# The eighth block's convolution in the short form, the permuted input weights loaded two blocks earlier, a row buffer cleared later

## The chip, the cores and the metric

The kernel runs on one core of a Trainium2 chip. A core has five engines that each work through their own instructions in order and meet at semaphores: TensorE (PE in the profile; PEld is its loading of weights), VectorE (DVE), ScalarE (ACT), GpSimd (POOL), and SyncE (SP), which here only issues DMAs. GpSimd issues DMAs too. Matrix products land in PSUM, from where ScalarE and VectorE carry them to SBUF. The metric is the device time of one execution in microseconds, the median over several runs.

## The reference

Two stages on 8 x 4096 tokens of 192 features (8 heads of 24). First a causal convolution whose 7 taps are given per token and head, after a softmax over the taps; then a two-layer network of width 2048 with a squared ReLU:

```python
w = softmax(weight_gen)                      # (B, S, 8 heads, 7 taps)
x_unf = x_pad[:, idx, :].reshape(B, S, 7, 8, 24)
y = einsum('bshk,bskhg->bshg', w, x_unf).reshape(B * S, 192)
h = maximum(y @ w_in, 0)                     # 32768 x 2048
out = (h * h) @ w_out                        # 32768 x 192
```

The result is float32; inside, the kernel computes in float16 with float32 sums.

## The kernel before

**Tiling.** The 32768 tokens are 64 tiles of 512. They go in 33 blocks (`BLOCKS`, L55), counted from 0: blocks 0 and 1 are one tile, all others two (block 7 is tiles 12 and 13). Batch row 1 begins with tile 8.

**Stages of a block.**

1. *Softmax.* Tap weights are worked on in parts of a batch row: eight, sixteen or thirty-two tokens on each of 128 partitions (`PARTS`, L102). A part is loaded (`load`, L209), then goes through in pieces: an exponential on ScalarE (`exp`, L239), and on VectorE a sum, a reciprocal and four or eight products into a row buffer (`soft`, L841, which calls `total`, `recip` and `scale`). Small parts use `v_first`, the others `v_big` (L103), in which each token's taps stand on the diagonal of an 8-token square and all else is zero; it must be cleared once before its first use. When a part's last piece is done, a small part is moved straight to the tiles' rows `wr` by DMAs on two queues (`move_rows`, L684); a larger one is stored to DRAM (`store`, L285) and loaded again as rows (`wr_load`, L354), which has to wait for the store.
2. *Bands.* `st_bands` (L665) multiplies a tile's rows by a mask on VectorE and makes a band matrix `bd` (some 2.3 us per tile).
3. *Convolution.* TensorE multiplies x by the bands. The long form (`st_conv`, L525) takes 120 matmuls, because heads of 24 features straddle groups of 32; both PSUM results are copied by ScalarE. The short form (`st_conv_spread`, L488) gives each of six heads its own group of 32 and puts the last two heads' features into the holes: 80 matmuls, one copy on ScalarE and one on VectorE, and then four small DMAs on SyncE that move rows within y (L523). The input weights then have to stand in the matching order: `w_p` in place of `w_i`. `FIRST_SPREAD` (L48) says from which block on the short form is used.
4. *Units.* `st_unit` (L578): 16 units u0 to u15 for each block, six matmuls each into a PSUM buffer; ScalarE applies ReLU, VectorE squares, two units at a time but for u14 and u15, which are squared singly (L603).
5. *Second product.* `st_mm2` (L618) in steps, eight a block (M0 to M7), each 32 matmuls over eight of the sixteen units. They lag: the steps in block j use the units of block j-1. An even step begins a pair of accumulators in PSUM, the odd one after it ends them, and `o_sum` (L646) brings them out: ScalarE copies one, VectorE adds the other. There is a single pair (`ps_o`, one buffer, L90), so the next even step can begin only when that sum is done. An odd M step reads units 8 to 15, the last of them at its end.

PSUM has three more buffers (`ps_h`, L89), which the units and both halves of a convolution take in turn.

**What sets the order.** Everything is emitted in an order written out by hand, and each engine keeps it. For blocks 0 to 3 the whole order is in `plans` (L762); for later blocks it comes from a pattern of letters: u is a unit, M a second-product step, C the convolution of the next block. The pattern is `steady` (L760) before a long convolution, `steady_spread` (L761) before a short one:

```python
steady = "MuMuuu" * 3 + "MuuuMCu"
steady_spread = "MuMuuu" * 2 + "MuCMuuu" + "MuMuuu"
```

Into it are put, each ahead of a given unit, softmax pieces (S, from `TIMES`, L779, as block and unit), their exponentials (E, `exp_time`, L788), loads (L) and bands (B, L811 to L818). What is ahead of u12 in the order is thus ahead of u12's square on VectorE. In plan 3, S3 ends the fourth part of batch row 0, and S4 begins the first part of row 1; B6 and B7 are block 4's bands.

**GpSimd's queue.** It holds the x loads (issued behind the convolution that frees their buffer, L896 to L900), half of the row moves (L368), the loads of `w_p` (`load_w_spread`, L151, 16 DMAs, in block 5 behind its x loads), two DMAs that cross the halves of `w_p` (`cross_w_spread`, L175, in block 6), and, in the opening, the memset of `v_big` (L755) between the x loads of tiles 2 and 3.

Of the kernel before, what the change touches and what calls it, by code (L numbers as in the profile page):

```python
# [9 lines left out]
def kernel(  # L10
# [26 lines left out]
    nc = tc.nc  # L37
# [7 lines left out]
    HK = H * KK  # L45
    G = D // H
    SPREAD = H - 2
    FIRST_SPREAD = 8  # L48
    HP = H // 2

    P = 128
# [51 lines left out]
    v_big = const.tile([P, R + 2 * HALO, HP, SL, 2], f16, name="v_big")  # L103
# [43 lines left out]
    def cross_w_in(q):  # L147
        for r0, r1 in ((0, RT), (RT, 0)):
            nc.sync.dma_start(out=w_i[r0 : r0 + RT, q, 1], in_=w_i[r1 : r1 + RT, q, 0])

    def load_w_spread():  # L151

        def rows(head, k=None):
            a = moe_w_in[G * head : G * (head + 1)]
            return a if k is None else a.rearrange("(r k) c -> k r c", k=NK)[k]

        for e in (0, 1):
            for k in range(NK):
                for a, n, src in (
                    (0, G, rows(2 * k + e)), (G, RT // 2 - G, rows(SPREAD + e, k))  # L160
                ):
                    if k < 2:
                        p0 = RT * k + 32 * e + a
                        nc.gpsimd.dma_start(
                            out=w_p[p0 : p0 + n, :, 0, 0:NQ],
                            in_=src.rearrange("r (q c) -> r q c", q=WQ),
                        )
                    else:
                        for half in (0, 1):
                            p0 = RT * half + 32 * e + a  # L170
                            nc.gpsimd.dma_start(
                                out=w_p[p0 : p0 + n, :, 0, NQ:],
                                in_=src.rearrange("r (q h c) -> h r q c", q=WQ, h=2)[half],
                            )
    def cross_w_spread():  # L175
        for r0, r1 in ((0, RT), (RT, 0)):
            nc.gpsimd.dma_start(out=w_p[r0 : r0 + RT, :, 1], in_=w_p[r1 : r1 + RT, :, 0])
# [158 lines left out]
    def x_load(j):  # L336
        x_t[j] = p_x.tile([P, NT, D], f16, name="xt")
        block_load(j, x_t[j], x[j // NBB], D, nc.gpsimd)
# [149 lines left out]
    def st_conv_spread(j):  # L488

        s0, n = BLOCKS[j]  # L490
        y = p_y.tile([P, NK + 1, TB], f16, name="y")
        y_t[j] = y
        for ks in ((NK, NK - 1), (0, 1)):
            yp = ps_h.tile([P, 2, TB], f32, name="yp", tag="h")
            k0 = min(ks)
            for k in ks:
                for i in range(NT):
                    a, b = bounds[i], bounds[i + 1]
                    for half in (0, 1):
                        s = s0 + half  # L500
                        hi = a + (STEP if tile_start(s, i) == starts[i] else b - a)
                        bd = bd_t[s][:, H * a : H * hi].rearrange(
                            "p (g c e) -> p g e c", g=HP, e=2
                        )
                        for e in (0, 1):
                            head = 2 * k + e
                            p0 = RT * half + 32 * e
                            c0 = min(G * head, D - 32)
                            nc.tensor.matmul(  # L509
                                out=yp[p0 : p0 + 32, k - k0, a:b],  # L510
                                lhsT=x_t[s][:, i, c0 : c0 + 32],
                                rhs=bd[:, head // 2, e, 0 : b - a],
                                start=True,
                                stop=True,
                                skip_group_check=True,
                                tile_position=(0, p0),
                            )
            copy = nc.vector.tensor_copy if k0 == 0 else nc.scalar.copy
            copy(out=y[:, k0 : k0 + 2], in_=yp)  # L519
        for p0 in range(0, P, 32):  # L520
            head = SPREAD + p0 // 32 % 2
            r0 = p0 + G * head - min(G * head, D - 32)
            nc.sync.dma_start(out=y[p0 + G : p0 + 32, 0:NK], in_=y[r0 : r0 + G, NK])  # L523

    def st_conv(j):  # L525

        if j >= FIRST_SPREAD:
            return st_conv_spread(j)
# [49 lines left out]
    def st_unit(j, u):  # L578

        w = w_p if j >= FIRST_SPREAD else w_i  # L580
        h = ps_h.tile([P, 2, TB], f32, name="h", tag="h")
# [83 lines left out]
    def st_bands(j):  # L665
        first = int(j % NBB == 0)
        last = NT - int(tile_start(j, NT - 1) != starts[-1])
        split = 2 if j == BLOCKS[NFIRST][0] else first
        for tiles in (range(first), range(first, split), range(split, last), range(last, NT)):
            if tiles:  # L670
                st_band(j, tiles)

    with nc.allow_low_precision("fp16 matmul pipeline"), tc.manual_schedule():
# [69 lines left out]
        def cast_w_in(e, copy):  # L743
# [8 lines left out]

        s2.load(nc.gpsimd)
        x_load(2)
        nc.gpsimd.memset(v_big, 0.0)  # L755

        steady = "MuMuuu" * 3 + "MuuuMCu"  # L760
        steady_spread = "MuMuuu" * 2 + "MuCMuuu" + "MuMuuu"  # L761
        plans = {  # L762
            0: "E1 u B1 u u u C S1 u u M u u",
            1: "L3 u u B2 M E2 B3 u u M E2 u S2 S2 u M u C u M",
            2: "L4 u u u E3 M u u u M B4 u u u u M B5 S3 u u u u M u C u",
            3: "L5 L6 u u E3 u M S3 u u u M u M E4 u u B6 u M u M B7 u u u E4 M u M C S4 u",
        }


# [3 lines left out]
        def at(j, u, kind, *args):  # L773
            fill.setdefault((j, u), []).append((kind, *args))
# [4 lines left out]
        TIMES = {  # L779
            (1, 0): ((3, 15), (4, 0)),  # L780
            (1, 1): ((4, 15), (5, 0)),
            (1, 2): ((4, 2), (5, 1), (5, 15)),
            (2, 0): ((6, 1), (6, 15), (7, 0)),
            (2, 1): ((7, 9), (8, 9)),
            (3, 0): ((9, 9), (10, 0), (10, 9), (11, 9)),
# [2 lines left out]
        def exp_time(j, u):  # L788

            if u == 0:  # L790
                return j - 1, 12
            return j, {1: 0, 2: 1, 7: 3, 8: 4, 9: 4, 13: 12, 15: 8}[u]

        for n, s in enumerate(parts):
            k = n - min(m for m, p in enumerate(parts) if p.b == s.b)
# [15 lines left out]
        for j in range(len(plans), NBLK - 1):  # L811
            a = BLOCKS[j + 1][0]
            small = [p for p in parts if p.fb <= j + 1][-1].r == FIRST
            us = {4: (7, 9), 6: (7, 9)}.get(j, (5, 9) if small else (1, 5))
            if j + 1 >= FIRST_SPREAD:
                us = (1, 5)
            for n, u in enumerate(us):
                at(j, u, "B", a + n)  # L818
        for j in range(len(plans), NBLK):
            plan, u = [], 0  # L820
            for step in steady_spread if j + 1 >= FIRST_SPREAD else steady:
                if step == "u":
                    plan += [f"{kind}{n}" for kind, n in fill.get((j, u), ())]
                    u += 1
                plan.append(step)
            plans[j] = " ".join(plan)
# [3 lines left out]
        def load_rows(j):  # L830

            s = [p for p in parts if p.fb <= j][-1]
            if s.r == FIRST:
                return
            if s in stored:
                for n in range(BLOCKS[j][0], sum(BLOCKS[j])):
                    wr_load(n)
            else:
                waiting.append((s, j))
# [40 lines left out]
        for j in range(NBLK):  # L880
            if j + 2 < NBLK:
                load_rows(j + 2)
            if j == 1:
                for q in range(WQ):
                    cross_w_in(q)
            u = 0
            for step in plans[j].split():
                kind, n = step[0], int(step[1:] or 0)
                if kind == "u":
                    st_unit(j, u)  # L890
                    u += 1
                elif kind == "M":
                    next(mm2)
                elif kind == "C" and j + 1 < NBLK:
                    st_conv(j + 1)
                    if j == 0:  # L896
                        x_load(3)
                    elif j + 2 < NBLK:
                        for k in range(BLOCKS[j + 2][0], sum(BLOCKS[j + 2])):
                            x_load(k)  # L900
                    if j == 5:
                        load_w_spread()
                    elif j == 6:
                        cross_w_spread()
                elif kind == "E":
                    parts[n].exp(*next(parts[n].exps))
                elif kind == "S":
                    soft(parts[n])
                elif kind == "B":
                    st_bands(n)  # L910
                elif kind == "L":
                    parts[n].load(nc.sync)


        j = NBLK - 1
# [44 lines left out]
```

## Time and profile before

| what | before |
|---|---|
| median of 6 runs | 730.03 us (729.86 to 732.21) |
| profiled execution | 730.17 us, its span 728.5 us |
| TensorE matmuls busy | 722.3 us, 99% of the span |
| weight loads busy | 530.9 us, 73% |
| VectorE busy | 625.8 us, 86% |
| ScalarE busy | 612.5 us, 84% |
| GpSimd busy | 99.5 us, 14% |
| granted TensorE clock | 0.999 of full speed |
| memset of the big row buffer | 2.49 us, from 17.65 us on |
| 6 long convolutions, matmuls | 120 each, in blocks 1 to 6 |
| 25 short convolutions, matmuls | 80 each, from 153.7 us on |

A line of the timeline has start, time, engine, source line, operation, what it writes and reads, shape and count; in brackets, how long the engine stood idle before it and what ended that. Instructions that follow each other alike are merged into one line. Times of one instruction overlap the next one's a little, so what an instruction costs its engine is best read from start to start. A busy TensorE in the table is not TensorE at its peak: ends of matmuls are modelled. Block 6 runs from 118.6 to 141.1 us, block 7 to 163.2.

### The profile page before, as it was taken

The page shows a single profiled execution, that of the slowest core. Times are in us where ns is not written, and L with a number is a line of the kernel's source. Part 1 is how long each engine was busy: PE and PEld are TensorE (multiplying, and loading weights), DVE is VectorE, ACT ScalarE, POOL GpSimd, SP SyncE. Part 2 cuts the span into 40 slices and gives each one's busy share as a digit, 9 for nine tenths or more (in the row PEclk, how much of TensorE's full clock was granted, in tenths as well). Part 3 has the DMA queues.
Part 4 walks back from the last instruction along what each step waited for, and adds up shares of the span by engine and source line. Part 5 has one row for each costly group of instructions (what it writes and reads, how often), then busy time and mean ns, then how long its engine had stood idle before and what let it go on. Part 6 is the DMA issues. An engine that isn't in the chain of part 4 may idle for free.

```text
span 728.5 us, 31057 instructions
## 1 busy us (share of the span) xinstructions
PE 722.3 (99%) x14082; PEld 530.9 (73%) x14082; DVE 625.8 (86%) x839; ACT 612.5 (84%) x731; POOL 99.5 (14%) x147
## 2 busy tenths in 40 slices
PE   8999999999999999999999999999999999999998
PEld 6668877777777777777777777777777777777777
DVE  7989997998898998888988888988888988778753
ACT  6898888888888888888888888888888888888883
POOL 6331223411001100011001010010000110001000
PEclk9999999999999999999999999999999999999999
DMA  9764455676245543356432554343544325444012
GB/s 186 136 115 105 81 125 90 128 142 138 77 72 132 105 76 69 73 116 125 85 60 59 133 104 88 68 73 110 115 76 87 57 55 115 67 87 78 29 46 67
DMA packets 127456, 68.30 MB, mean 94 GB/s; under 512 B 85449, under 2 KB 124060, under 8 KB 126812
## 3 DMA queue, kind: packets, MB, share of 16 engines
q1 hardware_dynamic: 80508, 47.19, 22.8%
q0 software_dynamic: 46672, 19.03, 22.6%
q8 instruction: 110, 1.80, 1.0%
q14 instruction: 22, 0.18, 0.1%
q10 hardware_dynamic: 144, 0.10, 0.0%
HBM read 50.18 MB, written 28.70 MB: 108 GB/s over the span
## 4 chain that ended last, share of the span: by engine, by line
PE 95%; DMA 2%; DVE 1%; issue 1%; POOL 1%; ACT 0%; SPq 0%; DVEq 0%; POOLq 0%
PE o L637 46%; PE h L588 44%; PE yp L509 4%; PE yp L543 1%; DMA xt<-in_x_dram 1%; DMA wr<-v_first 1%; DVE bd L413 0%; DMA wg<-in_weight_gen_dram 0%; POOL xt L328 0%; DVE rcp L265 0%; POOL w_o L190 0%; PE h L573 0%; DVE ssum L258 0%; POOL xt L334 0%; DVE v_first L273 0%
## 5 line engine op out<-in xcount | busy, mean ns | idle before, releaser
L602 ACT ACTIVATE t<-h 128x1024 f16<-128x1024 f32 x512 | 496.6, 1026 | 59.5 <-PE h L588 58.3
L637 PEld LDWEIGHTS <-g 64*128 64x128 f16 (+1 forms) x8032 | 344.6, 94 | 54.6 <-issue 1.9
L637 PE MATMUL o<-w_o,g 64*128 64x192 f16 (+1 forms) x8032 | 380.2, 243 | 0.0
L606 DVE TENSOR_TENSOR g<-t 128x2048 f16<-128x2048 f16 (+1 forms) x287 | 307.5, 1106 | 28.6 <-ACT t L602 28.2
L588 PE MATMUL h<-y,w_p 64*128 64x512 f16 x2400 | 291.8, 376 | 0.0
L588 PEld LDWEIGHTS <-w_p 64*128 64x128 f16 x2400 | 114.0, 94 | 94.7
L413 DVE TENSOR_TENSOR bd<-wr,mask 128x4160 f16<-128x4160 f16 (+4 forms) x90 | 149.5, 1686 | 1.4 <-ACT wr L398 0.7
L653 DVE TENSOR_TENSOR o_sb<-o,o_sb 128x384 f32<-128x384 f32 x123 | 68.5, 557 | 61.4 <-ACT o_sb L651 59.0
L334 POOL DMA_DIRECT2D xt<-in_x_dram x63 | 52.6, 839 | 415.4 <-PE yp L509 362.4
L651 ACT COPY o_sb<-o 128x384 f32<-128x384 f32 x129 | 61.6, 477 | 45.6 <-PE o L637 44.5
L588 PE MATMUL h<-y,w_i 64*128 64x512 f16 x576 | 70.8, 377 | 0.2 <-issue 0.2
L588 PEld LDWEIGHTS <-w_i 64*128 64x128 f16 x576 | 31.0, 94 | 21.7 <-issue 1.7
L509 PEld LDWEIGHTS <-xt 128*32 128x32 f16 x2000 | 24.4, 95 | 10.6 <-issue 10.6
L273 DVE TENSOR_TENSOR v_big<-ex,rcp 128x112 f16<-128x112 f32 (+5 forms) x180 | 29.9, 238 | 2.1 <-DMA vd<-v_big 1.1
L519 DVE CAST y<-yp 128x1024 f16<-128x1024 f32 x25 | 30.5, 1219 | 0.0
L509 PE MATMUL yp<-bd,xt 128*32 128x104 f16 (+1 forms) x2000 | 28.3, 209 | 0.0
L251 ACT ACTIVATE ex<-wg 128x560 f32<-128x560 f32 (+5 forms) x40 | 26.2, 656 | 1.5 <-DMA wg<-in_weight_gen_dram 1.4
L258 DVE TENSOR_REDUCE ssum<-ex 128x80 f32<-128x560 f32 (+5 forms) x40 | 25.6, 641 | 1.2 <-ACT ex L251 1.2
L519 ACT CAST y<-yp 128x1024 f16<-128x1024 f32 x25 | 25.2, 1007 | 0.0
L265 DVE RECIPROCAL rcp<-ssum 128x64 f32<-128x64 f32 (+4 forms) x39 | 23.0, 589 | 1.3
L324 POOL DMA_DIRECT2D xt<-in_x_dram x7 | 3.9, 555 | 120.3 <-PE yp L509 109.4
L368 POOL DMA_DIRECT2D wr<-v_first x24 | 13.0, 564 | 21.3 <-DVE v_first L273 21.1
(41 smaller groups left out, 113.7 us busy)
## 6 DMA issues: line engine op xcount, KB each, us to landing
out_dram<-o_sb SPq DMA_DIRECT2D x63, 384.0 KB
xt<-in_x_dram POOLq DMA_DIRECT2D x42, 240.0 KB, 4.8
wg<-in_weight_gen_dram SPq DMA_DIRECT2D x4, 1064.0 KB
xt<-in_x_dram POOLq DMA_DIRECT2D x21, 192.0 KB, 4.5
wr<-vd SPq DMA_DIRECT2D x38, 80.0 KB
vd<-v_big SPq DMA_DIRECT2D x5, 512.0 KB
y<-y SPq DMA_DIRECT2D x100, 24.0 KB
wg<-in_weight_gen_dram SPq DMA_DIRECT2D x3, 616.0 KB
```

The lines of the kernel that those rows point to most:

```text
L251: nc.scalar.activation(out=self.ex[:, lo:hi].rearrange("p r g k e -> p (r g) k e"), in_=self.wg[:, lo:hi].rearrange("p r (g e) k -> p (r g ...
L273: eng.tensor_tensor(out=bass.AP(tensor=v.tensor, offset=v.offset + lo * H * SL + lo % SL * 2 + g * SL * 2, ap=[list(v.ap[0]), [H * SL + 2, ...
L334: eng.dma_start(out=dst[:, first:last], in_=ap)
L413: nc.vector.tensor_tensor(out=bd_t[j][:, H * lo : H * (lo + len(tiles) * n)].rearrange("p (g m c) -> p g m c", g=shape[1], c=2 * SL), in0= ...
L509: nc.tensor.matmul(out=yp[p0 : p0 + 32, k - k0, a:b], lhsT=x_t[s][:, i, c0 : c0 + 32], rhs=bd[:, head // 2, e, 0 : b - a], start=True, sto ...
L519: copy(out=y[:, k0 : k0 + 2], in_=yp)
L588: nc.tensor.matmul(out=h[:, half], lhsT=w_in_chunk(w, u, slot, half), rhs=y_t[j][r0 : r0 + RT, k], start=(slot == 0), stop=(slot == NK - 1 ...
L602: nc.scalar.activation(out=t1[:, e], in_=h, func=ActF.Relu)
L606: nc.vector.tensor_tensor(out=g[:, a : e + 1], in0=t1[:, a : e + 1], in1=t1[:, a : e + 1], op=AluOp.mult)
L637: nc.tensor.matmul(out=oo[:, cc * Dm : (cc + 1) * Dm], lhsT=g[r0 : r0 + n, cc * P : (cc + 1) * P], rhs=w_o[r0 : r0 + n, fc, :], start=(fc ...
L651: nc.scalar.copy(out=o_sb, in_=o[0][:, c])
L653: nc.vector.tensor_tensor(out=o_sb, in0=o[1][:, c], in1=o_sb, op=AluOp.add)
```

## The change

`FIRST_SPREAD` goes from 8 to 7, so that block 7 (tiles 12 and 13) has the short convolution, and its units use `w_p`.

- Block 6, in which this convolution lies, gets a pattern of its own, `first_spread`: the convolution stands behind its tenth unit (u9) and not ahead of u15, and the block ends in M7 u13 u14 u15.
- Block 7's bands go from ahead of u7 and u9 of block 6 to ahead of u5 and u7.
- The last piece of part 6 (the large part whose rows these tiles need) goes from ahead of u15 to ahead of u12 of block 5. With it move the part's store and the row loads of tiles 12 and 13 on SyncE's queue. Its exponential stays ahead of u8.
- The 16 loads of `w_p` go from block 5 to block 3, behind S3 (letter W); the two crossing DMAs go from block 6 to block 5, behind its x loads. So GpSimd's queue has the 16 loads between the row moves of S3 and the x loads of block 5, and the crossing DMAs behind the x loads of block 7.
- The memset of `v_big` goes from the opening to block 1, behind the convolution of block 2 and the x loads of block 3.

```diff
-    FIRST_SPREAD = 8
+    FIRST_SPREAD = 7
...
         x_load(2)
-        nc.gpsimd.memset(v_big, 0.0)
...
+        first_spread = "MuMuuu" * 2 + "MuMuCuu" + "MuMuuu"
...
-            3: "L5 L6 u u E3 u M S3 u u u M u M E4 u u B6 u M u M B7 u u u E4 M u M C S4 u",
+            3: "L5 L6 u u E3 u M S3 W u u u M u M E4 u u B6 u M u M B7 u u u E4 M u M C S4 u",
...
-            (1, 2): ((4, 2), (5, 1), (5, 15)),
+            (1, 2): ((4, 2), (5, 1), (5, 12)),
...
-            return j, {1: 0, 2: 1, 7: 3, 8: 4, 9: 4, 13: 12, 15: 8}[u]
+            return j, {1: 0, 2: 1, 7: 3, 8: 4, 9: 4, 12: 8, 13: 12, 15: 8}[u]
...
             if j + 1 >= FIRST_SPREAD:
-                us = (1, 5)
+                us = (5, 7) if j + 1 == FIRST_SPREAD else (1, 5)
...
-            for step in steady_spread if j + 1 >= FIRST_SPREAD else steady:
+            form = first_spread if j + 1 == FIRST_SPREAD else steady_spread
+            for step in form if j + 1 >= FIRST_SPREAD else steady:
...
-                    if j == 5:
-                        load_w_spread()
-                    elif j == 6:
+                    if j == 1:
+                        nc.gpsimd.memset(v_big, 0.0)
+                    elif j == 5:
                         cross_w_spread()
...
+                elif kind == "W":
+                    load_w_spread()
```

## The prediction

> **What bounds the kernel now.** I read the busy times first, then the chain of waits, then the matmul engine's timeline around the ends of blocks 5 to 7, then the vector engine's timeline over the same stretch. Blocks count from 0, so the eighth is block 7. M0 to M7 are a block's eight second-matmul steps, u0 to u15 its units.
>
> The page, busy time by engine:
>
> ```profile
> PE 722.3 (99%) x14082; PEld 530.9 (73%) x14082; DVE 625.8 (86%) x839; ACT 612.5 (84%) x731; POOL 99.5 (14%) x147
> ```
>
> TensorE is never free for long, so its own work and the holes cut into it are the time. The chain of waits agrees: from 33 us on it runs through TensorE alone, but for one hole of 0.24 us. Before that, it passes through the Pool queue:
>
> ```profile
> 17.65 0.22 POOL v_big L755
> 17.87 2.16 issue
> 20.04 0.61 POOL xt L328
> 20.64 0.71 POOL xt L334
> 21.35 3.94 DMA wr<-v_first
> ```
>
> The memset of the big row buffer stands ahead of x loads and of the row moves for which the first two-tile conv waits.
>
> TensorE's timeline (start, time, line): the end of block 5 (M7, long conv, u15, M0 of block 6), then the short conv inside block 7.
>
> ```profile
> 114.97 1.50 PE L637 MATMUL o<-w_o,g 64*128 64x192 f16 x32
> 116.40 1.58 PE L543 MATMUL yp<-bd,xt 128*32 128x104 f16 x120
> 117.92 0.82 PE L588 MATMUL h<-y,w_i 64*128 64x512 f16 x6
> 118.58 1.48 PE L637 MATMUL o<-w_o,g 64*128 64x192 f16 x32
> ...
> 153.65 1.14 PE L509 MATMUL yp<-bd,xt 128*32 128x104 f16 x80
> 154.72 1.49 PE L637 MATMUL o<-w_o,g 64*128 64x192 f16 x32
> ```
>
> From start to start an M step takes 1.32 us and a unit 0.65. Nothing waits at 118.58.
>
> VectorE's timeline (start, time; in brackets idle and releaser):
>
> ```profile
> 113.22 2.35 DVE L606 TENSOR_TENSOR g<-t 128x2048 f16<-128x2048 f16 x2
> 115.87 1.83 DVE L606 TENSOR_TENSOR g<-t 128x2048 f16<-128x2048 f16 x2 [0.29 <-ACT t L602]
> 117.61 0.55 DVE L653 TENSOR_TENSOR o_sb<-o,o_sb 128x384 f32<-128x384 f32 x1
> 118.08 0.49 DVE L258 TENSOR_REDUCE ssum<-ex 128x48 f32<-128x336 f32 x1
> ...
> 130.15 2.32 DVE L413 TENSOR_TENSOR bd<-wr,mask 128x4160 f16<-128x4160 f16 x1
> 132.38 1.22 DVE L606 TENSOR_TENSOR g<-t 128x2048 f16<-128x2048 f16 x1
> ...
> 140.69 0.62 DVE L258 TENSOR_REDUCE ssum<-ex 128x64 f32<-128x448 f32 x1
> ...
> 142.68 0.69 DVE L606 TENSOR_TENSOR g<-t 128x1024 f16<-128x1024 f16 x1
> ...
> 163.19 2.52 DVE L606 TENSOR_TENSOR g<-t 128x2048 f16<-128x2048 f16 x3 [0.38 <-ACT t L602]
> ```
>
> The reader should see that VectorE, only 86% busy on average, is packed here and runs in the order written: squares, then M7's sum, then the softmax piece, then u15's square. M0 of the next block reuses the two accumulators that M7's sum reads, so this sum gates TensorE. Its slack was 118.58 - 118.16 = 0.42 us.
>
> **The gains.** *Short form.* Before, M7 to u15 takes 117.92 - 114.97 = 2.95 us; less 1.32 for M7, the long conv costs 1.63. The short one costs 154.72 - 153.65 = 1.07 and 0.09 of gap ahead of it, 1.16. Gain 0.47.
> *Memset.* Its 2.49 us leave the Pool queue at 17.65, so the two x loads behind it start that much sooner. The conv that waits took 31.34 - 29.51 = 1.83 us from its start to the next unit, against 117.92 - 116.40 = 1.52 unheld: there is 0.31 to win, and 0 if the row moves land no sooner, since earlier loads keep the DMA engines busy until 24 us. VectorE waited 0.65 us for the rows, and this conv needs only 0.31 of it, so I take 0.31.
>
> **The holds.** *1, M0 of block 6.* The piece of part 6 goes from behind M7's sum to ahead of u12's squares: 118.08 to 119.81, 1.73 us. It eats the idle 0.29 and the slack 0.42; M0 is held for 1.73 - 0.71 = 1.02.
> *2, the moved conv.* Its second band now stands ahead of u7, and the conv behind u9. From M3's end (127.10 in the old times), ScalarE's copy ends at 127.78; then VectorE does the sum (0.47 to the next start), a band (2.24), squares (1.14) and a band (2.32), to 133.98. TensorE is there after u5 to u7, M4, u8, M5, u9: 1.94 + 1.32 + 0.65 + 1.32 + 0.65 and 0.09, at 133.07. With 0.04 to release (a band's end at 29.99, the conv's start at 30.03), the hold is 0.95.
> *3, u12 of block 6.* The short form casts one half on VectorE (1.22 us; the long one cast both on ScalarE), and u12 needs that PSUM buffer. Behind the band come squares, sum, squares, cast: 1.14 + 0.47 + 1.14 + 1.22 after 133.91, so 137.88. TensorE: 134.02 + 1.05 + two units + M6 = 137.69. Hold 0.23.
> *4, M1 of block 7.* Block 6 now ends in M7 u13 u14 u15 with a softmax piece ahead of u15's square. Take block 7's tail, which has this order without the piece: with T = 163.22 (next M0), the squares start at T - 0.03, u12/13 take 1.14, u14 0.60. Add the piece (140.69 to 142.68, 1.99) and u15's square 0.69: T + 4.39. M1 reads it in the last eighth: 1.32 + 0.65 + 1.16 = T + 3.13. Hold 1.26 + 0.04 = 1.30. In the old order the piece lay beside the conv and the square was done by 143.37, with M1 needing it at 144.26.
> *5, M2 of block 7.* Behind that square stands another piece (1.74), then M1's sum, on which M2 waits: some 0.10.
>
> **Costed at nothing.** The 16 weight loads (0.58 us each, 9.3 on the Pool queue) go behind the row moves that end at 61.77, ahead of x loads at 72.74, whose conv starts at 93.45. If they slow the last row move (issued at 62.19) to the 5.5 us that a store beside them took (119.87 to 125.36), rows land at 67.7 for a band at 67.34: 0.3, most of it slack. The two crossing DMAs (1.31 on the queue, 7.5 to land) start near 120 for a use at 143. The memset goes behind x loads that end at 39.93; Pool's next work is at 51.12 and the buffer's first write at 80.91. On SP, part 6's store and two row loads go ahead of M7's output store: at most 5.5 + 1.1 us behind 117.3, for a buffer rewritten at 132.5. Rows for band 12 land by 117.3 + 5.5 + 4 = 126.8, before 128.3; VectorE's wait of 1.05 on that store goes, into idle time. The four y copies (3.0 us of SP issue behind the cast, some 4 to land) give about 143.3 for u0 of block 7 at 144.1; if they took the 7.2 us of the store issued at 145.04 beside the crossing DMAs, u0 waits 1.9, but hold 4 shrinks by 1.3: 0.6 more.
>
> The memset beside VectorE: in its old place the scale steps started every 0.185 us, during it and after it alike: cost 0. The upper end from rows: squares due at 40.75 stand until the memset's end at 42.43, 1.69 late; the next conv's slack is 0.5 (49.25 less 48.75), so 1.2. I take 0, the row nearest to it. The Trainium skill (SBUF — State Buffer, Terms) says of the port pair that VectorE and GpSimd share that "the loser fully blocks"; by this sentence the sum would be 1.2 us higher; the same page (Who interferes with whom) exempts two-input vector work against a GpSimd instruction that only writes, but no row here has such 16-bit work beside a memset.
>
> **Sum.** 1.02 + 0.95 + 0.23 + 1.30 + 0.10 - 0.47 - 0.31 = +2.82 us. The profiled execution took 730.17 (span 728.5 and 1.7 around it), 0.14 above the median: 730.17 + 2.82 = 732.99, or 732.9 against the median 730.03. What a measurement can tell from no change is 0.2%, 1.46 us: beyond 731.49 is slower.
>
> **Rivals.**
> *A, the holds are hidden.* If VectorE issued the moved piece and bands when convenient and not in the written order, only the gains stay: 730.03 - 0.78 = 729.3, no slower. For it: VectorE idles 1.85 us at 121, and no row shows TensorE waiting for VectorE after 33 us. Against it: at 117.6 to 120.0 it keeps the written order while u15's square waits. It decides if the holds sum to under 2.24 us.
> *B, the DMAs or the memset add to it.* y copies 0.6, memset 1.2, rows 0.3, up to 735.0. For it: the DMA engines were full at 120 to 132, beside these weight loads. Against: that load leaves this stretch.
> *C, the short form saves nothing,* held to the long one's 1.63 by something new: 733.4. Against it: all 25 short convs are alike.
>
> **How the numbers follow.** Forecast 0.74, A 0.15 (mostly within 0.2%), B 0.09, C 0.02. One of the three large holds failing gives 731.6 to 732.0, so low is 731.0, a little into A; high is 735.0, B's end. Faster 0.03, same 0.12, slower 0.85.
>
> **What would show it.** Right: TensorE idle near 1 us at block 6's M0 with VectorE's sum as releaser, 0.95 in the short conv for a band, 1.3 in block 7's M1 for a square; block 8 starts 3 us late, and later blocks are unchanged. Wrong: M0 of block 6 starts straight behind u15, or the second band ends before u9.

## The result, and the profile after

The changed kernel takes 732.6 us (median of 17 runs, 731.88 to 733.95); the kernel before, beside it, 730.55 (37 runs, 729.67 to 732.97). The ratio is 1.0026 with a 95% interval of 1.0019 to 1.0034: slower by 1.9 us, between 1.4 and 2.5. The forecast was 2.8, to 732.9.

The profiled execution took 733.08 us with a span of 731.4. From the page of the changed kernel, the busy times by engine:

```profile
PE 723.2 (99%) x14042; PEld 533.2 (73%) x14042; DVE 627.0 (86%) x840; ACT 612.1 (84%) x730; POOL 99.1 (14%) x147
```

The busy shares in this line do not show the loss: TensorE is as full as before, with 40 matmuls fewer. The view of waits shows it. Before, it had no line in which the convolution or the second product waits for VectorE; now it has (engine and line, waited for, us in total, times, longest):

```profile
PE o L637 <- DVE o_sb L653: 1.5, 2, 0.8
PEld L637 <- DVE g L606: 1.4, 1, 1.4
PE o L637 <- DVE g L606: 1.1, 1, 1.1
PE yp L509 <- DVE bd L413: 0.7, 1, 0.7
```

Of the two waits in the first line, one lies in block 3 and is taken up with the last two experiments. Where the others lie, in TensorE's timeline of the changed kernel (start, time, operation, in brackets idle and releaser):

```profile
118.31 0.82 PE L588 MATMUL h<-y,w_i 64*128 64x512 f16 x6
118.97 0.24 PE L637 MATMUL o<-w_o,g 64*128 64x192 f16 x1
119.88 1.48 PE L637 MATMUL o<-w_o,g 64*128 64x192 f16 x31 [0.67 <-DVE o_sb L653]
121.13 0.87 PE L588 MATMUL h<-y,w_i 64*128 64x512 f16 x6
...
133.56 0.87 PE L588 MATMUL h<-y,w_i 64*128 64x512 f16 x6
134.36 0.22 PE L509 MATMUL yp<-bd,xt 128*32 128x104 f16 x2
135.25 1.12 PE L509 MATMUL yp<-bd,xt 128*32 128x104 f16 x78 [0.67 <-DVE bd L413]
136.31 1.53 PE L588 MATMUL h<-y,w_i 64*128 64x512 f16 x12
137.66 1.50 PE L637 MATMUL o<-w_o,g 64*128 64x192 f16 x32
139.12 0.82 PE L588 MATMUL h<-y,w_i 64*128 64x512 f16 x6
...
145.00 1.33 PE L637 MATMUL o<-w_o,g 64*128 64x192 f16 x28
147.47 0.34 PE L637 MATMUL o<-w_o,g 64*128 64x192 f16 x4 [1.14 <-DVE g L606]
147.65 2.11 PE L588 MATMUL h<-y,w_p 64*128 64x512 f16 x18
...
166.44 1.48 PE L637 MATMUL o<-w_o,g 64*128 64x192 f16 x32
```

Each step is read from start to start against its free time. Block 6's M0 takes 121.13 - 118.97 = 2.16 us for 1.32 (0.84 lost): after one matmul on the first accumulator it stands until the second is out. From u9 to the end of the conv are 136.31 - 133.56 = 2.75 for 0.65 + 0.09 + 1.07 = 1.81, that is 0.94 lost: only the first two matmuls, which need no more than the first tile's band, went ahead. M6 to u12 is 1.46 for 1.32, 0.14 lost. M1 of block 7 is 2.65 for 1.32, 1.33 lost, with all but its last four matmuls done: those read u15.

The counterpart in VectorE's timeline of the changed kernel:

```profile
115.88 0.50 DVE L258 TENSOR_REDUCE ssum<-ex 128x48 f32<-128x336 f32 x1
116.41 0.45 DVE L265 RECIPROCAL rcp<-ssum 128x48 f32<-128x48 f32 x1
116.90 0.72 DVE L273 TENSOR_TENSOR v_big<-ex,rcp 128x84 f16<-128x84 f32 x4
117.53 1.82 DVE L606 TENSOR_TENSOR g<-t 128x2048 f16<-128x2048 f16 x2
119.27 0.55 DVE L653 TENSOR_TENSOR o_sb<-o,o_sb 128x384 f32<-128x384 f32 x1
...
132.88 2.32 DVE L413 TENSOR_TENSOR bd<-wr,mask 128x4160 f16<-128x4160 f16 x1
...
137.85 1.22 DVE L519 CAST y<-yp 128x1024 f16<-128x1024 f32 x1
...
144.75 0.61 DVE L258 TENSOR_REDUCE ssum<-ex 128x64 f32<-128x448 f32 x1
145.40 0.55 DVE L265 RECIPROCAL rcp<-ssum 128x64 f32<-128x64 f32 x1
145.99 0.83 DVE L273 TENSOR_TENSOR v_big<-ex,rcp 128x112 f16<-128x112 f32 x4
146.73 0.69 DVE L606 TENSOR_TENSOR g<-t 128x1024 f16<-128x1024 f16 x1
```

The softmax piece now stands ahead of M7's sum (119.27, ends 119.82, M0 goes on at 119.88); the second band ends at 135.20 and the conv goes on at 135.25; the cast of the conv's second half ends at 139.07 and u12 starts at 139.12; u15's square ends at 147.42 behind the second piece, and M1 goes on at 147.47.

TensorE's timeline of the kernel before, at the start of block 8:

```profile
163.22 1.48 PE L637 MATMUL o<-w_o,g 64*128 64x192 f16 x32
```

From block 6's M0 to block 8's, the profile of before needs 163.22 - 118.58 = 44.64 us, that of the changed kernel 166.44 - 118.97 = 47.47. The difference of 2.83 is the four holds, 0.84 + 0.94 + 0.14 + 1.33 = 3.25, less the 0.47 of the short form, to within 0.05. This stretch is used below to compare kernels, because the times alone scatter by more than a single hold.

### The profile page after: what moved, and what is told of

The parts are those of the page before. It is cut to its first block, busy times and chain, and to the rows that moved or that the text cites. A ratio compares the mean times of both kernels' runs of the same rounds, so it can differ in the third digit from the quotient of the medians.

```text
span 731.4 us, 30985 instructions
## 1 busy us (share of the span) xinstructions
PE 723.2 (99%) x14042; PEld 533.2 (73%) x14042; DVE 627.0 (86%) x840; ACT 612.1 (84%) x730; POOL 99.1 (14%) x147
## 4 chain that ended last, share of the span: by engine, by line
PE 92%; DVE 5%; ACT 1%; DMA 1%; issue 1%; POOL 0%; DVEq 0%
PE o L637 45%; PE h L588 41%; PE yp L509 4%; DVE g L606 2%; PE h L573 2%; DVE bd L413 1%; PE yp L543 1%; DMA wr<-v_first 1%; ACT t L602 1%; DVE ssum L258 0%; DVE rcp L265 0%; DVE v_first L273 0%; PE pr L390 0%; PE yp L473 0%; DMA wg<-in_weight_gen_dram 0%
## 5 line engine op out<-in xcount | busy, mean ns | idle before, releaser
L588 PE MATMUL h<-y,w_p 64*128 64x512 f16 x2496 | 303.4, 376 | 0.0
L588 PEld LDWEIGHTS <-w_p 64*128 64x128 f16 x2496 | 118.6, 94 | 98.4
L588 PE MATMUL h<-y,w_i 64*128 64x512 f16 x480 | 59.7, 377 | 0.0
L588 PEld LDWEIGHTS <-w_i 64*128 64x128 f16 x480 | 28.1, 94 | 16.4 <-issue 1.7
```

The source lines that it names most:

```text
L588: nc.tensor.matmul(out=h[:, half], lhsT=w_in_chunk(w, u, slot, half), rhs=y_t[j][r0 : r0 + RT, k], start=(slot == 0), stop=(slot == NK - 1 ...
```

## The experiments

Theory: VectorE, full and working in written order, hands over late at these places, and that is the loss. Rivals: the moved transfers (the row loads, the store of part 6, the two crossing DMAs) are late, or the moved memset and weight loads cost something of their own. Each kernel was timed beside the kernel before, whose medians were 730.40 for the first four runs, 730.61 for the next four and 730.51 for the last two.

**Weight loads alone, in the kernel before.** The loads go to block 3, the crossing to block 5; nothing else moves.

```diff
-            3: "L5 L6 u u E3 u M S3 u u u M ...
+            3: "L5 L6 u u E3 u M S3 W u u u M ...
...
-                    if j == 5:
-                        load_w_spread()
-                    elif j == 6:
+                    if j == 5:
                         cross_w_spread()
```

> The kernel before with one part of the change: the 16 loads of w_p in block 3 behind S3 and the crossing in block 5; long convolution, pieces, bands and memset as before. In the changed kernel TensorE was held 0.85 us in block 3, at M6, by a sum that stood on VectorE behind a band whose rows came late (rows issued at 58.45 landed at 63.26, 4.8 us, against 2.8 before). Theory that the weight loads slow these row moves: the hold shows here too, VectorE idles 0.5 to 1.0 us before block 4's first band, block 4's first M step begins 0.6 to 1.0 us later than in the profile of before, and the time is 0.6 to 1.0 us above the kernel before; nothing else moves. Rival, that the rows land late from the earlier clock of the opening or by chance: no hold here, time within 0.3 us of the kernel before.

Measured: 731.19 us (10 runs), ratio 1.0009 (1.0000 to 1.0018). The hold in block 3 is not there. What is new stands elsewhere: blocks 6 and 7 take 45.71 us. In VectorE's timeline of this run, a scale step (a product into the row buffer) waits for the store of that buffer, and band 12 (the band of tile 12) for its rows:

```profile
127.11 0.83 DVE L273 TENSOR_TENSOR v_big<-ex,rcp 128x112 f16<-128x112 f32 x4 [1.91 <-DMA vd<-v_big]
...
132.31 2.33 DVE L413 TENSOR_TENSOR bd<-wr,mask 128x4160 f16<-128x4160 f16 x1 [0.50 <-DMA wr<-vd]
```

Both theories on block 3 missed that. With the piece of part 6 still ahead of u15, its store stands behind two x loads, as in the kernel before, and the crossing now stands beside its rows.

**Memset alone, in the kernel before.**

```diff
-        nc.gpsimd.memset(v_big, 0.0)
...
                     if j == 5:
                         load_w_spread()
+                    if j == 1:
+                        nc.gpsimd.memset(v_big, 0.0)
```

> The kernel before with the memset of the row buffer alone moved to block 1. Theory: the first two-tile convolution is no longer held (its 120 matmuls in 1.5 us and not 1.9), all later M steps begin 0.3 to 0.45 us earlier, the time is 0.3 to 0.45 us below the kernel before, VectorE's 16-bit work beside the memset keeps its length (squares 1.22 us, bands 2.32). Rival, that the two engines block one another at their shared port: a square or band beside the memset starts or ends up to 1.7 us late. Rival for block 3's hold: if it comes from the earlier opening and not from the weight loads, block 3's M6 is held here.

Measured: 730.48 us (11 runs), ratio 0.9996 (0.9987 to 1.0005): a gain of 0.3 us is not excluded, nor is none. In this trace the hold of the first two-tile conv did not go: the conv takes 2.01 us. Its VectorE timeline shows the bands still waiting for rows, longer than the 0.65 us of before:

```profile
25.41 4.67 DVE L413 TENSOR_TENSOR bd<-wr,mask 128x1664 f16<-128x1664 f16 x4 [0.82 <-DMA wr<-v_first]
```

**Part 6's piece put back.**

```diff
-            (1, 2): ((4, 2), (5, 1), (5, 12)),
+            (1, 2): ((4, 2), (5, 1), (5, 15)),
```

> The changed kernel with the last piece of part 6 put back ahead of u15 of block 5. VectorE theory: the hold of block 6's M0 (0.84 us) goes, M7's sum ends before u15 does; what is late next is the part's store, some 2.3 us later, and with it the rows of block 7's tiles. If the rows still come in time (issue to landing below 4 us) the time falls by 0.8 us against the changed kernel. Rival, that the transfers set the limit there: in the changed kernel the row load issued at 120.9 landed after 127 (6 us or more) beside x loads and the crossing; 2.3 us later it lands after 129.5, band 12 waits 0.5 to 2.5 us for it, and the convolution's hold grows from 0.94 by as much, so that little or nothing is won.

Measured: 736.22 us (4 runs), ratio 1.0076 (1.0057 to 1.0094), 3.6 us above the changed kernel. M0 of block 6 is free, but the rival came true, and more strongly than expected: the conv's hold grows from 0.94 to 3.41 us (132.65 to 137.87, less 1.81), and blocks 6 and 7 take 49.22 us. The two traces so differ by 1.75 us; where the rest of the 3.6 lies is not known, since the profiled execution (734.85) was the fastest of the four. SyncE's timeline of the changed kernel:

```profile
117.69 0.32 SPq L287 DMA_DIRECT2D vd<-v_big  x1
120.91 0.94 SPq L334 DMA_DIRECT2D wr<-vd  x2
121.94 0.83 SPq L658 DMA_DIRECT2D out_dram<-o_sb  x1
```

and VectorE's of the same kernel:

```profile
129.51 2.32 DVE L413 TENSOR_TENSOR bd<-wr,mask 128x4160 f16<-128x4160 f16 x1
```

SyncE's timeline of the kernel with the piece put back:

```profile
118.42 0.39 SPq L658 DMA_DIRECT2D out_dram<-o_sb  x1
120.11 0.34 SPq L287 DMA_DIRECT2D vd<-v_big  x1
125.86 1.51 SPq L334 DMA_DIRECT2D wr<-vd  x3
```

and VectorE's of it:

```profile
125.80 0.83 DVE L273 TENSOR_TENSOR v_big<-ex,rcp 128x112 f16<-128x112 f32 x4 [1.31 <-DMA vd<-v_big]
...
131.08 2.33 DVE L413 TENSOR_TENSOR bd<-wr,mask 128x4160 f16<-128x4160 f16 x1 [1.71 <-DMA wr<-vd]
```

The row loads wait on SyncE for the store to land, so the distance from the store's line (`vd<-v_big`) to the first row load is the store's time. Issued ahead of the two x loads (118.7) it took 3.2 us; issued 2.4 us later, behind them, 5.7. There it also stands behind M7's output store (`out_dram`, 384 KB), which in the changed kernel comes after it. The x loads themselves landed 7.4 us after their issue there, and 4.5 in the changed kernel. No run separates the x loads from the output store. So the move of this piece costs 0.84 us at M0, and in this order it saves more than that at the conv.

**Part 7's second piece ahead of u12.**

```diff
-            (2, 0): ((6, 1), (6, 15), (7, 0)),
+            (2, 0): ((6, 1), (6, 12), (7, 0)),
```

> The changed kernel with the second piece of part 7 ahead of u12 of block 6 and not ahead of u15. VectorE theory: the 2.0 us piece falls into VectorE's idle 1.43 + 0.65 us before and after M7's sum, u15's square ends by T + 2.5 us (T the start of block 7's M0), M1 of block 7 is not held, and the time is 1.1 to 1.35 us below the changed kernel; M0 of block 7 is held by at most 0.2 us. Rival, that M1 waits for something else at that place (weights, y rows): its hold of 1.3 us stays.

Measured: 731.43 us (10 runs), ratio 1.0007 (0.9998 to 1.0016), 1.2 us below the changed kernel's median. Blocks 6 and 7 take 46.14 us, 1.33 less, which is the size of the hold. TensorE's timeline of this run at the same M1, now in one piece of 1.32 us:

```profile
144.78 1.50 PE L637 MATMUL o<-w_o,g 64*128 64x192 f16 x32
146.10 2.12 PE L588 MATMUL h<-y,w_p 64*128 64x512 f16 x18
```

This settles the cause of the largest hold: one line in the order, with the same work and the same transfers, takes it away.

**The conv two units later, without VectorE's copy,** on top of the run before.

```diff
-            copy = nc.vector.tensor_copy if k0 == 0 else nc.scalar.copy
+            copy = nc.vector.tensor_copy if k0 == 0 and j != FIRST_SPREAD else nc.scalar.copy
...
-        first_spread = "MuMuuu" * 2 + "MuMuCuu" + "MuMuuu"
+        first_spread = "MuMuuu" * 2 + "MuMuuuC" + "MuMuuu"
```

> The changed kernel with part 7's second piece ahead of u12 (as in the run before that did so), block 7's convolution behind u11 and not u9, and both its PSUM copies on ScalarE. VectorE theory: TensorE reaches the convolution 1.3 us later, after the second band is done, so the hold of 0.94 us there goes, and so does u12's 0.14 since no copy stands behind VectorE's squares; only block 6's M0 is still held, 0.8 us. Blocks 6 and 7 together cost 0.3 to 0.5 us more than in the profile of before (0.84 less 0.47), the time is 1.0 to 1.2 us below the run with the piece alone and 0.1 to 0.5 above the kernel before. Rival, that the y rows or the ring of PSUM buffers set the limit: block 7's u0, or u12 or u13 of block 6, is held by 0.5 to 1.5 us in their place.

Measured: 731.95 us (10 runs), ratio 1.0014 (1.0005 to 1.0023), no gain. The waits for the band and at u12 are gone from the trace; yet blocks 6 and 7 take 46.07 us, 0.07 less. TensorE's timeline:

```profile
134.72 1.46 PE L509 MATMUL yp<-bd,xt 128*32 128x104 f16 x80
136.11 1.49 PE L637 MATMUL o<-w_o,g 64*128 64x192 f16 x32
...
141.35 1.48 PE L637 MATMUL o<-w_o,g 64*128 64x192 f16 x32
143.03 1.13 PE L588 MATMUL h<-y,w_p 64*128 64x512 f16 x6 [0.19 <-DMA y<-y]
```

The conv takes 1.39 for 1.07: its second half takes, by the order of the three buffers, the PSUM buffer of u10; ScalarE's ReLU of u10 ends at 135.47, and the conv's weight loads pause at 135.25 and go on at 135.52. And u0 of block 7 comes 1.68 us after M0 instead of 1.32, waiting for the y rows. The rival was right: with the hold by VectorE gone, two new ones of about the same size took its place.

**Part 6's piece back, and the crossing in block 4.** The edit of the run with the piece put back, and:

```diff
+        at(4, 7, "X", 0)
...
-                    elif j == 5:
-                        cross_w_spread()
...
+                elif kind == "X":
+                    cross_w_spread()
```

> The kernel of the run with part 6's piece put back ahead of u15 of block 5, with the two crossing DMAs moved to block 4 (ahead of u7), where no other transfer waits. Transfer theory: the crossing next to the x loads is what made store and rows late there; now the store lands within 3 us, the rows within 4, band 12 waits for nothing, the convolution's hold is 0.9 to 1.0 us as in the changed kernel and M0's is gone: 0.8 us below the changed kernel, about 3.5 us below that run. Rival, that the x loads alone are enough to delay them: VectorE still waits 0.5 us or more for the store and for the rows.

Measured: 733.16 us (5 runs), ratio 1.0035 (1.0023 to 1.0048), 3.1 us below the run with the piece put back, but not below the changed kernel. Blocks 6 and 7 take 48.22 us, 1.00 less than in that run. Without the crossing, band 12 no longer waits for rows: asked for from 126.00 us on, they let it start at 129.49; with the crossing they were asked for from 125.86 on, and it started at 131.08. The store still takes from 119.53 to 126.00 behind the x loads, and VectorE stands for it:

```profile
125.94 0.83 DVE L273 TENSOR_TENSOR v_big<-ex,rcp 128x112 f16<-128x112 f32 x4 [2.03 <-DMA vd<-v_big]
```

So each half of the two theories holds in these traces: the crossing delays the rows, and the store is late without it, behind the x loads and M7's output store.

**All repairs together.** The edits of the last three runs: piece of part 6 ahead of u15, crossing in block 4, piece of part 7 ahead of u12, conv behind u11 with both copies on ScalarE.

> All repairs at once: part 6's piece ahead of u15 of block 5, the crossing in block 4, part 7's second piece ahead of u12, the convolution behind u11 with both copies on ScalarE. VectorE theory: no hold of more than 0.2 us in blocks 5 to 7; block 6 takes 22.1 us from M0 to M0 (22.55 in the kernel before), the short form's 0.47 us is kept, and the time is 0.3 to 0.8 us below the kernel before. Rival, that the short form's saving is taken by something else than these holds: block 6 stays at 22.5 us or more.

Measured: 730.61 us (11 runs), ratio 1.0000 (0.9991 to 1.0009): level with the kernel before, 2 us below the changed one. Blocks 6 and 7 take 45.13 us. M0 of block 6, M1 of block 7 and u12 are free; what remains are 0.34 us in the conv and some 0.6 in block 7 at the y rows, which the expectation had not allowed for.

**The conv one unit earlier again,** otherwise as the last.

```diff
-        first_spread = "MuMuuu" * 2 + "MuMuuuC" + "MuMuuu"
+        first_spread = "MuMuuu" * 2 + "MuMuuCu" + "MuMuuu"
```

> The run with all three repairs, with the convolution behind u10 in place of u11. There the convolution lost 0.32 us to a PSUM buffer that ScalarE had not freed, and block 7 lost 0.6 us from u0 on, which waited for the y rows (copied on SyncE from 138.1, u0 due at 142.6). One unit earlier: TensorE comes 0.3 us before the second band is done, so the convolution is held 0.3 us; the buffers are free; the y rows are asked for some 1.0 us sooner and u0 of block 7 is not held. Blocks 6 and 7 together take 44.4 to 44.7 us (44.64 in the profile of before, 45.13 with all three repairs, 47.47 in the changed kernel), the time is equal to the kernel before or up to 0.5 us below. Rival, that the y rows need the 0.6 us whatever their start (their transfers wait behind x loads): u0 is held as before.

Measured: 730.60 us (11 runs), ratio 1.0004 (0.9994 to 1.0013). Block 7's u0 no longer waits for the y rows and the conv loses 0.38, as expected, but blocks 6 and 7 take 45.12 us. TensorE's timeline shows block 7's M0 held in their place:

```profile
141.16 0.24 PE L637 MATMUL o<-w_o,g 64*128 64x192 f16 x1
141.74 1.48 PE L637 MATMUL o<-w_o,g 64*128 64x192 f16 x31 [0.34 <-DVE o_sb L653]
```

The squares ahead of the piece waited 1.20 us for ScalarE, which now has both copies of the conv, and the piece then stands ahead of M7's sum (it ends at 141.69): the same kind of hold as at block 6's M0. No order tried brings these two blocks below the 44.64 us of the long form, which took 44.99 in the trace with the memset alone.

**The changed kernel again, and with the loads behind block 4's bands.** The first is one more run of the same kernel; the second moves W in plan 3 from behind S3 to behind B7.

> The changed kernel once more, for the hold of 0.85 us at M6 of block 3. If the weight loads cause it, it is there again with 0.5 to 1.0 us. If it is scatter in the landing of the row moves (their margin in the profile of before was 0.24 us), it is absent or below 0.3 us, while the holds of blocks 6 and 7 (0.84, 0.94, 0.14, 1.33) come back within 0.1 us.

> The changed kernel with the 16 weight loads behind block 4's second band, some 8 us later in block 3. If they delay S3's row moves, the 0.6 to 0.85 us hold at block 3's M6 (seen in two profiles of the changed kernel, not in five others with the loads at the same place) does not appear and the time is up to 0.4 us below the changed kernel. If that hold is scatter of the row moves, it can appear here as well, and the time is that of the changed kernel, 732.6 within 0.5. The holds of blocks 6 and 7 stay: 0.84, 0.94, 0.14 and 1.33 us.

Measured: the repeat took 734.7 us in its one run, the other 732.94 (5 runs), ratio 1.0034 (1.0022 to 1.0046). Blocks 6 and 7 took 47.46 and 47.44 us: the holds return to a few hundredths. Block 3 was held again in the repeat (0.60 us) and not with the loads moved. VectorE's timeline of the changed kernel there:

```profile
64.07 2.33 DVE L413 TENSOR_TENSOR bd<-wr,mask 128x4160 f16<-128x4160 f16 x1 [0.91 <-DMA wr<-v_first]
```

and TensorE's of the same kernel:

```profile
68.05 1.48 PE L637 MATMUL o<-w_o,g 64*128 64x192 f16 x31 [0.85 <-DVE o_sb L653]
```

Of the nine traces that have the loads directly behind S3, two show this hold; of the three without, none. That does not decide between the loads and scatter, and moving them brought no time, so it stays open.

## Why the prediction was right, and where it was off

**Hold 1, M0 of block 6:** 1.02 predicted, 0.84 measured, the same in the repeat. M0's first matmul uses the accumulator that ScalarE frees and went ahead, and the sum came a little earlier. The step that called the wait on SP harmless held.
**Hold 2, the moved conv:** 0.95 predicted, 0.94 measured, by the chain that was summed.
**Hold 3, u12:** 0.23 predicted, 0.14 measured.
**Hold 4, M1 of block 7:** 1.30 predicted, 1.33 measured, and removed alone by one line.
**Hold 5, M2 of block 7:** 0.10 predicted, nothing measured (149.59 - 147.65 = 1.94, three units at full pace).
**Short form:** 0.47 predicted. It was not isolated, but the stretch closes to 0.05 with it.

The stretch of blocks 6 and 7 was so put at +3.13 and came at +2.83. The other 0.6 between 2.8 forecast and 1.9 measured has less certain sources. The trace that was summed stood at 730.17, 0.4 below the median of 37 runs of the same kernel, though the prediction put it 0.14 above; and in the run with the memset alone, whose order there is that of before, blocks 6 and 7 took 44.99 us and not 44.64. TensorE lost 0.16 us there in three units (from 127.16 us) and 0.16 in the long conv (from 139.18), and the profile names nothing that it waited for. So the kernel before can be slower in this stretch; why and how often stays open. That the forecast time of 732.9 came within 0.3 us of the measured 732.6 is in part luck: it started from a median 0.5 us below the later one and added 0.8 us too much.

**Memset:** 0.31 was taken. The mechanism is there in part: of ten traces with the memset moved, six have the first two-tile conv unheld (1.5 us), four still have it held (1.8 to 2.25), as have both without the move (1.83 and 2.01). The lower bound, a gain of 0 because the rows come too late all the same, is what happened in those four; the step that failed is that the hold goes each time.

**The memset beside VectorE** cost nothing, as taken. GpSimd's timeline of the changed kernel:

```profile
39.22 2.56 POOL L903 MEMSET v_big<- 128x2816 f16 x1
```

and VectorE's of the same kernel:

```profile
40.31 1.23 DVE L606 TENSOR_TENSOR g<-t 128x2048 f16<-128x2048 f16 x1 [0.61 <-ACT t L602]
41.45 2.32 DVE L413 TENSOR_TENSOR bd<-wr,mask 128x4160 f16<-128x4160 f16 x1
```

The square waits for ScalarE as before and both run their usual length with the memset beside them. The sentence of the Trainium skill (SBUF — State Buffer, Terms) that "the loser fully blocks", read by itself, would have held the square until 41.78; this row goes against that reading. It agrees with the narrower sentence of the same page (Who interferes with whom), which leaves out a GpSimd instruction that only writes.

**Rival A** needed holds below 2.24 us; they were 3.25 in the trace. **Rival B** got a small part at most: the y rows were in time, and the block 3 hold appeared in two traces. **Rival C** is not borne out: the stretch closes only with the 0.47 us of the short form taken off. **What the prediction did not see** is that the piece's move was worth more than it cost: it put the store at 5.5 us in its new place on SyncE, where it took 3.2. It saw that VectorE's wait of 1.05 us on the store goes, but not what the old place would cost with the crossing beside it: waits of 1.31 us for the store and 1.71 for the rows.

## What to carry to other kernels

When a step is moved on an engine that runs in written order, list what now stands behind it and the consumer of each; the slack of that one handover decides, and an engine that is 86% busy on average can have none there. A saving of 0.47 us on TensorE is only kept if every handover near it keeps its slack: here removing holds brought out the next ones, a PSUM buffer, y rows, another sum, and the best order only drew level. Where single holds are smaller than the scatter of the whole time, compare one stretch between two marks of the trace, and take more than one trace of a stretch in which transfers decide.

## What the runs showed beside this

The opening scatters from run to run: in the twelve traces the first two-tile conv starts between 29.24 and 31.12 us. In four of them TensorE was held 0.47 to 1.61 us behind an exponential that waited 0.72 to 1.86 us for a load of tap weights, issued at 6.7 us. ScalarE's timeline of the repeat of the changed kernel:

```profile
13.57 0.94 ACT L251 ACTIVATE ex<-wg 128x784 f32<-128x784 f32 x1 [1.86 <-DMA wg<-in_weight_gen_dram]
```

and TensorE's of the same run:

```profile
15.46 0.93 PE L573 MATMUL h<-y,w_i 64*128 64x512 f16 x4 [1.61 <-ACT t L602]
```

In the profile of before, ScalarE waited 0.25 us there and TensorE not at all; in the run with the weight loads alone, TensorE was held 1.17. The exponential stands ahead of the ReLUs on ScalarE, so the late load reaches TensorE at once. The largest of these is longer than any of the four holds. It accounts for the distance between the two profiled executions of the changed kernel: 1.62 us in time (734.7 and 733.08), and 1.56 already at block 6's M0 (120.53 and 118.97). Whether it also makes the spread of some 2 us among the runs without a trace is not shown.

The same store, behind the same two x loads and M7's output store and with no crossing near it, made VectorE wait 2.03 us in the run with the crossing in block 4 and 0.51 in the run with all repairs. The Trainium skill (DMA: Bandwidth & Descriptors, Issuing engines are not separate DMA queues) says that DMAs of all issuing engines interleave on the same 16 DMA engines. The store's 3.2 us ahead of GpSimd's x loads and 5.7 behind them fit this, but do not show it alone, since M7's output store, which SyncE issues itself, changed its place with them.
